# A talking-heads attention with an expert layer: every PSUM place as a tile of its own, given out by the list schedule

## The chip, the cores and the metric

The kernel runs on one core of one Trainium2 chip. The metric is the device time of one execution in microseconds (us); lower is better. A core has five engines with queues of their own: TensorE (PE, matrix products, with its weight loads shown apart as PEld), VectorE (DVE), ScalarE (ACT), GpSimd (POOL) and SyncE (SP, which issues the transfers here). PE writes its products to PSUM, from where DVE and ACT take them; the kernel lays PSUM out as eight banks of 512 fp32 values in each of 128 partitions.

## What is computed

Four batches, 12 heads, 448 tokens, 64 values to a head, and then a feed-forward layer over all 1792 tokens:

```python
scores = scale * np.matmul(q, k.transpose(0, 1, 3, 2))
scores = np.einsum('bhij,hg->bgij', scores, w_pre)
scores = scores - np.max(scores, axis=-1, keepdims=True)
attn = np.exp(scores)
attn = attn / (np.sum(attn, axis=-1, keepdims=True) + 1e-09)
attn = np.einsum('bhij,hg->bgij', attn, w_post)
x = np.matmul(attn, v)          # then (token, head * 64)
...
h = x @ w_in                    # 768 -> 2048
relu6 = np.clip(h + 3.0, 0.0, 6.0)
g = h * relu6 / 6.0
out = g @ w_out                 # 2048 -> 768
```

The two einsums mix the 12 heads before and after the softmax.

## The kernel before

A batch's 448 query rows are cut into chunks of 120, 120, 120 and 90 rows. The work on PE comes in these kinds:

- **scores** (line 327): for each pair of heads, queries times keys into the double bank `pqk`, six pairs to a chunk; ACT copies them out (line 358) and they go through DRAM into the mixing layout `T_all`.
- **pre** (line 421, in `step`): a step is 20 query rows (10 in the last step of a short chunk), as two halves r = 0 and 1 of ten rows. Each half mixes the heads of its scores into one bank of `pp`. DVE takes the row maximum (428), ACT the exponential (429), POOL and DVE the normalization (431, 432, 437). From the second batch on the result is split into two fp16 parts (443, 445, 446).
- **post** (line 455): mixes the heads again, one product group for each half r: 24 matmuls of 60 columns in fp16, 8 in fp32 in the first batch. Both halves use the same place `po`, which is the left halves of two banks of `pz`. ACT evicts half 0 (466) and DVE half 1 (464) into `A`, in runs of five values.
- **av** (492): `A` times the values at a chunk's end, into a double bank of the same ring as the scores' (`pav`).
- **moe1** (612): the first layer of the expert part, 16 groups of 18 matmuls for each of eight token groups (240 or 208 tokens), into one of three half banks of `pz`; ACT (622) and DVE (624) evict a group.
- **across** (272, 274): small reductions over partitions, in another part of `pz`.
- **moe2** (759): the second layer, 24 groups of 48 matmuls, into the banks of `pp`; ACT evicts (764).

The order of all instructions is worked out when the program is built. `Plan` takes every operation with an engine, an estimated duration, what it reads and writes, and a priority; `run` is a list scheduler that goes through estimated time and, whenever an engine is free, takes the ready operation of the best priority. Operations of moe1 and moe2 have late priorities and fill what the others leave. Each engine then executes its list strictly in that order, and waits for what the tiles' readers and writers require. Which place in PSUM a product uses is set before the scheduler runs, by counters (`half`, `bank`) and rings. PSUM has three tiles: `pz` (three banks), `pp` (three banks) and the double bank of `pqk` and `pav`:

```python
    pz = const([P, 3, 2, 256], F32, "pz", psm)
    pp = const([P, 3, 512], F32, "pp", psm)
    banks, wide = [3], [True]
    HALVES = [(2, 0), (0, 1), (2, 1)]
```

For the scheduler each place inside `pz` and `pp` is a buffer of its own (`shared`); for the waits that the program is built with, `pz` is one tile and `pp` is one tile.

Of the kernel before, what the change touches and what calls it, by code (L numbers as in the profile page):

```python
# [48 lines left out]
class Op:  # L49
    __slots__ = ("eng", "dur", "fn", "prio", "n", "succ", "order", "ready", "end", "bytes", "no", "mode")  # L50


class Buf:


    def __init__(self, make, ring=None):
        self.make, self.t, self.uses = make, None, []
        self.prev = self.old = None
# [17 lines left out]

class Plan:
# [11 lines left out]
    def op(self, eng, dur, fn, r=(), w=(), prio=0.0, after=(), nbytes=0, mode=0):  # L89
        o = Op()  # L90
        o.eng, o.dur, o.fn, o.prio, o.bytes, o.mode = eng, dur, fn, prio, nbytes, mode
        o.succ, o.order, o.n, o.ready, o.no = [], [], 0, 0.0, len(self.ops)
# [29 lines left out]
    def run(self):  # L122
# [10 lines left out]
        bw, mode = 0.0, None  # L133
        for o in self.ops:
            if o.eng not in free:
                free[o.eng], wait[o.eng], ready[o.eng] = 0.0, [], []
            if o.n == 0:
                heapq.heappush(wait[o.eng], (0.0, o.no, o))

        def release(s, t):  # L140
            s.ready = max(s.ready, t)
            s.n -= 1
            if s.n == 0:
                heapq.heappush(wait[s.eng], (s.ready, s.no, s))

        while True:
            best = None
            for e in free:
                if ready[e]:
# [10 lines left out]
            while wait[e] and wait[e][0][0] <= t + 1e-9:  # L160
                o = heapq.heappop(wait[e])[2]
                heapq.heappush(ready[e], (o.prio, o.no, o))
            o = heapq.heappop(ready[e])[2]
            if e == "PE" and o.mode != mode:
                same = [x for x in ready[e] if x[2].mode == mode and x[0] < o.prio + self.STAY]
                if same:
                    ready[e].remove(min(same))
                    heapq.heapify(ready[e])
                    heapq.heappush(ready[e], (o.prio, o.no, o))
                    o = min(same)[2]  # L170
# [20 lines left out]
def body(ctx: ExitStack, tc: tile.TileContext, q4, kT, vj, wpre0, wpost0, ident0, w_in, w_out, outT):  # L191
# [55 lines left out]
    HALVES = [(2, 0), (0, 1), (2, 1)]  # L247
    turn = [0]
# [563 lines left out]
```

## Time and profile before

| | before |
|---|---|
| time, median of 3 runs | 1128.89 us (1128.63 to 1132.57) |
| time of the profiled execution | 1122.48 us |
| its span, first to last instruction | 1120.7 us |
| PE busy | 920.3 us (82%) |
| PE weight loads | 682.4 us (61%) |
| ACT, DVE, POOL busy | 476.0 us (42%), 465.6 us (42%), 369.4 us (33%) |
| granted TensorE clock, mean | 0.941 of full speed |

An engine is busy while an instruction of it is shown to execute; the end of a matmul is modelled. PE is the busiest engine by far, but the share is an average over stages that work differently: attention with moe1 between it (to about 755 us), moe1 alone (755 to 855 us), and moe2 (855 us to the end).

### The profile page before, as it was taken

To read this page: it belongs to the slowest core of one execution; us is meant where nothing else is said; L and a number is where in the kernel's file an instruction comes from. 1 tells how busy PE (TensorE), PEld (TensorE's weight loads), DVE (VectorE), ACT (ScalarE), POOL (GpSimd) and SP (SyncE) were. 2 spreads that over 40 slices of the span, in tenths; PEclk is the share of its full clock that TensorE was granted. 3 is DMA by queue.
4 is the path that set the end of the run, shared out by engine and by line. 5 is a ranking of instruction groups with operands and counts; after the bars stand their busy time and mean duration, and the time that the engine had idled before them with its cause. 6 is when DMAs were issued, how large, how long until landed. Compare 5 with 4: busy or idle time off the path is not lost.

```text
span 1120.7 us, 25096 instructions
## 1 busy us (share of the span) xinstructions
PE 920.3 (82%) x10492; PEld 682.4 (61%) x10492; DVE 465.6 (42%) x961; ACT 476.0 (42%) x926; POOL 369.4 (33%) x529
## 2 busy tenths in 40 slices
PE   6878898787887887898887896776668999999997
PEld 1445455554554654555664555665557888888887
DVE  4455656565446367467475565323211020110300
ACT  3454556465556466467564464423212230211200
POOL 1332434166545364466464364512002400000000
PEclk8586789999999999999998999879999999999999
DMA  7785477465466678677776563034213331220300
GB/s 206 200 257 148 148 206 238 140 199 167 107 197 180 186 209 245 185 235 211 230 209 200 172 202 110 18 122 150 69 40 101 97 117 65 78 87 33 115 17 33
DMA packets 80936, 166.07 MB, mean 148 GB/s; under 512 B 7416, under 2 KB 51544, under 8 KB 80824
## 3 DMA queue, kind: packets, MB, share of 16 engines
q1 hardware_dynamic: 80824, 164.48, 49.1%
q8 instruction: 82, 1.34, 0.5%
q14 instruction: 30, 0.25, 0.1%
HBM read 99.27 MB, written 62.60 MB: 144 GB/s over the span
## 4 chain that ended last, share of the span: by engine, by line
PE 56%; ACT 10%; DVE 10%; issue 4%; POOL 1%; DMA 1%; SPq 0%; ACTq 0%; DVEq 0%; POOLq 0%
PE pp L759 22%; PE pz L612 19%; PE pav L492 5%; PE pz L455 4%; ACT rl L622 3%; PE pqk L327 3%; DVE g L624 3%; PE pp L421 2%; ACT e L429 2%; ACT A L466 2%; DVE A L464 2%; DVE nb L428 2%; ACT o L764 1%; DVE eh L443 1%; ACT x L497 1%
## 5 line engine op out<-in xcount | busy, mean ns | idle before, releaser
L612 PE MATMUL pz<-x,wi 128*128 128x208 f16 (+1 forms) x2304 | 254.3, 267 | 60.7 <-DVE g L624 47.2
L612 PEld LDWEIGHTS <-wi 128*128 128x128 f16 x2304 | 218.3, 100 | 103.4 <-issue 91.2
L759 PE MATMUL pp<-g,wo 128*128 128x448 f32 x1152 | 244.3, 372 | 16.9 <-ACT o L764 16.9
L759 PEld LDWEIGHTS pp<-g,wo 128*128 128x128 f32 x1152 | 219.6, 192 | 41.3 <-ACT o L764 25.2
L446 POOL TENSOR_TENSOR el<-e,eh 128x448 f16<-128x448 f32 x135 | 144.2, 1076 | 109.6 <-ACT eh L445 82.9
L437 POOL TENSOR_SCALAR e<-e,r 128x448 f32<-128x448 f32 x180 | 128.4, 725 | 66.6 <-DVE r L432 63.2
L429 ACT ACTIVATE e<-pp,nb 128x448 f32<-128x448 f32 x173 | 108.7, 631 | 70.2 <-DVE nb L428 53.4
L622 ACT ACTIVATE rl<-pz,three,uh 128x240 f32<-128x240 f32 (+1 forms) x128 | 68.8, 537 | 142.6 <-PE pz L612 80.7
L327 PE MATMUL pqk<-ks,qx 64*64 64x448 f32 (+1 forms) x744 | 121.1, 603 | 6.2 <-ACT s L358 5.4
L624 DVE SCALAR_TENSOR_TENSOR g<-rl,six,pz 128x240 f32<-128x240 f32 (+1 forms) x128 | 56.7, 443 | 160.2 <-ACT rl L622 99.6
L455 PEld LDWEIGHTS <-eh 60*128 60x128 f16 x2160 | 57.0, 94 | 108.4 <-issue 107.0
L428 DVE TENSOR_REDUCE nb<-pp 128x1 f32<-128x448 f32 x173 | 101.9, 614 | 35.0 <-ACT e L429 19.6
L421 PE MATMUL pp<-T_all,wpre 64*64 64x448 f32 (+1 forms) x692 | 99.6, 585 | 19.2 <-ACT e L429 10.4
L455 PE MATMUL pz<-wpost_h,eh 60*128 60x60 f16 x1080 | 62.1, 190 | 59.6 <-DVE g L624 23.6
L749 DVE TENSOR_TENSOR g<-gr,g 128x896 fp32r<-128x896 f32 x32 | 34.6, 1091 | 181.4 <-ACT g L748 181.4
L464 DVE TENSOR_SCALAR A<-pz 128x480 f32<-128x480 f32 x88 | 60.0, 682 | 116.2 <-ACT rl L622 63.0
L466 ACT ACTIVATE A<-pz 128x480 f32<-128x480 f32 x92 | 59.8, 650 | 110.4 <-PE pz L612 78.3
L358 ACT ACTIVATE s<-pqk 120x896 f32<-120x896 f32 (+1 forms) x90 | 82.2, 914 | 20.0 <-PE pqk L327 6.8
L455 PEld LDWEIGHTS pz<-wpost_n,e 60*128 60x128 f32 x720 | 55.0, 227 | 46.6 <-issue 24.9
L764 ACT ACTIVATE o<-pp,uo 128x448 f32<-128x448 f32 x24 | 15.1, 634 | 159.0 <-PE pp L759 159.0
L492 PE MATMUL pav<-A,v 128*64 128x120 f32 (+1 forms) x1536 | 81.0, 265 | 1.4 <-ACT A L466 0.7
L492 PEld LDWEIGHTS pav<-A,v 128*64 128x64 f32 x1536 | 76.2, 140 | 5.5 <-issue 2.3
(96 smaller groups left out, 868.4 us busy)
## 6 DMA issues: line engine op xcount, KB each, us to landing
T_all<-sd SPq DMA_DIRECT2D x82, 420.0 KB, 4.5
sd<-s SPq DMA_DIRECT2D x66, 420.0 KB, 5.9
gr<-gd SPq DMA_DIRECT2D x32, 448.0 KB, 3.5
wi<-in_w_in SPq DMA_DIRECT2D x16, 768.0 KB, 4.4
wo<-in_w_out SPq DMA_DIRECT2D x24, 512.0 KB, 8.6
gd<-g SPq DMA_DIRECT2D x32, 240.0 KB, 2.9
sd<-s SPq DMA_DIRECT2D x24, 315.0 KB, 4.9
gd<-g SPq DMA_DIRECT2D x32, 208.0 KB, 3.4
```

Source lines behind the costliest of these rows:

```text
L327: PE.matmul(at[u]()[c:c + m], q()[r, pr, c:c + m], k()[r, pr % 3, :], start=True, stop=True)
L421: PE.matmul(ps[r]()[64 * u:64 * u + 64, :S], wpre8()[rows], T_all()[rows, slot, u], start=True, stop=True)
L428: dve(0.67, lambda r=r: DVE.tensor_reduce(nb()[:, r:r + 1], ps[r]()[:, :S], axis=AX.X, op=ALU.max, negate=True), [ps[r]], [(nb, r)], s + 0 ...
L429: act(0.87, lambda r=r: ACT.activation(e()[:, r], ps[r]()[:, :S], AF.Exp, bias=nb()[:, r:r + 1], accum_out=sm()[:, r:r + 1]), [ps[r], (nb, ...
L437: pool(0.73, lambda r=r: POOL.tensor_scalar(e()[:, r], e()[:, r], rr()[:, r:r + 1], 1.0, op0=ALU.mult, op1=ALU.mult), [rr], [(e, r)], s + ...
L446: pool(1.05, lambda r=r: POOL.tensor_tensor(el()[:, r], e()[:, r], eh()[:, r], op=ALU.subtract), [(e, r), (eh, r)], [(el, r)], s + 0.7 + 0 ...
L455: PE.matmul(pz()[:, u, 0, jc * HR:jc * HR + HR], x()[rows, r, js], w()[rows], start=(i == 0), stop=(i == len(mix) - 1))
L492: PE.matmul(ps()[u * D:(u + 1) * D, run, k:k + n], v()[:, jc, g * D:(g + 1) * D], a()[:, jc * H + g, :n], start=(jc == 0), stop=(jc == NJ ...
L612: PE.matmul(pv(), wi_g[g]()[:, w, f0, cc, :], x()[:, z, cc, :n], start=(cc == 0 and i == 0), stop=(cc == 5 and i == 2))
L622: act(0.57, lambda fc=fc, pv=pv, r=r: ACT.activation(r()[:, :n], pv(), AF.Relu, bias=three()[:, fc:fc + 1], scale=uh()[:, fc:fc + 1]), [ps ...
L624: dve(0.5, lambda fc=fc, pv=pv, r=r, gt=gt: DVE.scalar_tensor_tensor(gt()[:, fc % 2, :n], r()[:, :n], six()[:, fc:fc + 1], pv(), op0=ALU.m ...
L759: PE.matmul(ps()[:, :S], woh[e]()[:, w, fc, :], gs[b, k]()[:, z, fc % 2, :], start=(fc == 0 and i == 0), stop=(fc == NFC - 1 and i == 2))
```

## The change

`Places` is a set of PSUM tiles: one double bank (`pair0`) for the scores and six single banks (`single0` to `single5`) for everything else. A product that needs a place no longer has one assigned by a counter. It says from which set it takes, the scheduler counts it as available only when enough places of the set are free in estimated time, and takes the place that came free first. PE's choice among ready operations is rewritten around that; its rule to stay with the same kind of product within a margin of priority is kept.

Some products change with it. A step's two post halves become one operation that writes two single banks, one for the upper and one for the lower rows (u = 0 and 1); a matmul's 60 results now go to twelve runs of five values with gaps of five between (the other half's values), where they went to 60 adjacent values. ACT evicts the one bank and DVE the other, each when the whole operation is done, in runs of ten. The two halves of an av product and each moe1, moe2 and across product take a single bank of their own. Some entries are added to what a product reads and writes (`(e, "pe")`, `(a, (t, 2))`, `rx`, `(uh, fc)`): in the scheduler's count it then also waits for the buffers that its evictions read or write.

```diff
+class Places:
+
+
+    def __init__(self, makes):
+        self.makes, self.held = makes, [None] * len(makes)
+
+    def free_at(self, i, hop):
+        b = self.held[i]
+        if b is None:
+            return 0.0
+        ends = [u.end for _, u, _ in b.uses]
+        return None if None in ends else max(ends) + hop
+
+    def ready(self, k, hop):
+        t = sorted(x for x in (self.free_at(i, hop) for i in range(len(self.held))) if x is not None)
+        return t[k - 1] if len(t) >= k else None
+
+    def take(self, b, hop):
+        i = min((x, i) for i, x in ((i, self.free_at(i, hop)) for i in range(len(self.held))) if x is not None)[1]
+        self.held[i] = b
+        b.make = self.makes[i]
+
+            if b.pool and not b.uses and b not in o.takes:
+                o.takes.append(b)
...
+        def avail(o):
+            t = o.ready
+            for p in {b.pool for b in o.takes}:
+                x = p.ready(sum(b.pool is p for b in o.takes), self.HOP)
+                if x is None:
+                    return None
+                t = max(t, x)
+            return t
...
+            if e == "PE":
+                at = [(avail(x[2]), x) for x in ready[e]]
+                at = [x for z, x in at if z is not None and z <= t + 1e-9]
+                x = min(at)
+                x = min([z for z in at if z[2].mode == mode and z[0] < x[0] + self.STAY] or [x])
+                ready[e].remove(x)
+                o = x[2]
+                for b in o.takes:
+                    b.pool.take(b, self.HOP)
+            else:
...
-    pz = const([P, 3, 2, 256], F32, "pz", psm)
-    pp = const([P, 3, 512], F32, "pp", psm)
-    banks, wide = [3], [True]
-
-    def shared(ring):
-        return Buf(None, rings.setdefault(("shared", ring), Ring(1)))
-
-    def half():
-        turn[0] = (turn[0] + 1) % len(HALVES)
-        return shared(("ph", turn[0])), HALVES[turn[0]]
-
-    def bank(name):
-        k = banks[0] = (banks[0] + 1) % (4 if wide[0] else 3)
-        z = shared(("pp", k))
-        z.make = (lambda: pz()[:, 2].rearrange("p a b -> p (a b)")) if k == 3 else lambda: pp()[:, k]
+    pairs = Places([const([P, 2, 512], F32, f"pair{i}", psm) for i in range(1)])
+    singles = Places([const([P, 512], F32, f"single{i}", psm) for i in range(6)])
+    mixed = singles
+
+    def place(places):
+        z = Buf(None)
...
+        ps = [place(mixed) for r in range(R)]
...
+        pe(0.85, pre, [T, wpre8], [*ps, (e, "pe")], s - 0.7, mode=1)
...
-            po = shared(("po", 0))
...
+        po = [place(mixed) for u in range(2)]
+        w = G5 * R
+
+        def post():
+            for r in range(R):
...
-                            PE.matmul(pz()[:, u, 0, jc * HR:jc * HR + HR], x()[rows, r, js], w()[rows], start=(i == 0), stop=(i == len(mix) - 1))
+                            out = po[u]()[:, :NJ * H * w].rearrange("p (j g r i) -> p j r g i", j=NJ, g=H, r=R)[:, jc, r]
+                            PE.matmul(out, x()[rows, r, js], z()[rows], start=(i == 0), stop=(i == len(mix) - 1))
+
+        pe(dur * R, post, [x for x, _ in mix] + [z for _, z in mix], [*po, (a, (t, 2))], s + 1.2, mode=2)
+        far = G5 * R
+        for u in range(2):
+            def view(u=u, a=a):
+                return po[u]()[:, :NJ * H * w].rearrange("p (x y) -> p x y", y=w), a()[:, :, i0 + u * far:i0 + u * far + w]
+
+            if u:
+                dve(0.68, lambda view=view: DVE.tensor_scalar(view()[1], view()[0], 2.0 ** -28, None, op0=ALU.mult), [po[u]], [(a, (t, u))], s + 1.4)
             else:
+                act(0.62, lambda view=view: ACT.activation(view()[1], view()[0], AF.Copy, scale=2.0 ** -28), [po[u]], [(a, (t, u))], s + 1.4)
...
+            ps = place(singles)
...
+            pe(2.5, mm, [a, v, rx], [ps, (x, ("pe", c % 2, run))], at + 4 * run, mode=5)
...
-            ps, z = half()
-            pv = lambda z=z: pz()[:, z[0], z[1], :n]
+            ps = place(singles)
+            pv = lambda ps=ps: ps()[:, :n]
...
-            pe(0.0079 * n, mm, [x, *[(wi_g[g], (k, fc)) for k in range(3)]], [ps], at + fc,
-               [u for _, u, _ in rings["shared", ("pp", 3)].all[-1].uses] if (G, fc) in ((0, 0), (0, 1), (0, 2)) else ())
+            pe(0.0079 * n, mm, [x, (uh, fc), *[(wi_g[g], (k, fc)) for k in range(3)]], [ps], at + fc)
...
-        ps = bank(f"po_{b}_{e}")
+        ps = place(singles)
```

Three places show how the order of instructions moves. In the names, `single_84` and the like are the single banks with a running number of the buffer.

The first is PE in the first batch's attention. Before, the post of one step (the rows with `e_424`, eight matmuls for each half) and between its halves a reduction and a score product:

```order
L455 MATMUL pz<-wpost_n,e_424 128x60 x8
L274 LDWEIGHTS ones
L274 MATMUL pz<-top_wi_505,ones 128x1
L327 MATMUL pqk_2_2_536<-ks_0_97,qx_2_168 64x448 x2
L327 MATMUL pqk_2_2_536<-ks_0_97,qx_2_168 56x448 x2
L455 MATMUL pz<-wpost_n,e_424 128x60 x8
```

And after, the last four post matmuls of a step and what follows, the pre product of other steps (`T_all`):

```order
L496 MATMUL single_84<-wpost_n,e_326 128x12x5
L496 MATMUL single_127<-wpost_n,e_326 128x12x5
L458 MATMUL single_156<-T_all,wpre_148 64x448 x2
L458 MATMUL single_136<-T_all,wpre_148 64x448 x2
L458 MATMUL single_154<-T_all,wpre_148 64x448 x2
L458 MATMUL single_134<-T_all,wpre_148 64x448 x2
L309 LDWEIGHTS wist_427
L309 MATMUL single_84<-ident,wist_427 1x128
```

The two halves no longer stand apart with other products between them, the post alternates between two banks, and the pre products and a reduction go to other single banks.

The second is ACT near the end of moe1, where the `rl` of one group follows another. Before:

```order
L622 ACTIVATE rl_8_10800<-pz,three,uh_8254 128x240
L622 ACTIVATE rl_9_10825<-pz,three,uh_8254 128x240
L622 ACTIVATE rl_10_10847<-pz,three,uh_8254 128x240
L622 ACTIVATE rl_11_10869<-pz,three,uh_8254 128x240
L622 ACTIVATE rl_12_10891<-pz,three,uh_8254 128x240
```

And after:

```order
L662 ACTIVATE rl_2_10571<-single_156,three,uh_7792 128x240
L662 ACTIVATE rl_3_10591<-single_84,three,uh_7792 128x240
L662 ACTIVATE rl_4_10615<-single_134,three,uh_7792 128x240
L662 ACTIVATE rl_5_10637<-single_127,three,uh_7792 128x240
L662 ACTIVATE rl_6_10659<-single_136,three,uh_7792 128x240
L662 ACTIVATE rl_7_10681<-single_154,three,uh_7792 128x240
L662 ACTIVATE rl_8_10703<-single_156,three,uh_7792 128x240
```

Each group was read from `pz`; now six banks take turns, and a bank comes back at the seventh group.

The third is PE in moe2, where one pair of groups (`wo_10457`, `wo_10575`) ends and the next begins, with the semaphores that a row waits for. Before:

```order
L759 MATMUL pp<-g_7_12440,wo_10457 128x448 x3
L759 MATMUL pp<-g_7_12440,wo_10575 128x448 x3
L759 MATMUL pp<-g_0_12278,wo_11358 128x448 [waits Activation_49]
L759 MATMUL pp<-g_0_12278,wo_11358 128x448 x2
L759 MATMUL pp<-g_0_12278,wo_11408 128x448 [waits Activation_49]
L759 MATMUL pp<-g_0_12278,wo_11408 128x448 x2
L759 MATMUL pp<-g_0_12278,wo_11358 128x448 x3
```

And after:

```order
L798 MATMUL single_156<-g_7_12340,wo_10137 128x448 x3
L798 MATMUL single_84<-g_7_12340,wo_10273 128x448 x3
L798 MATMUL single_134<-g_0_12178,wo_11258 128x448 x3
L798 MATMUL single_127<-g_0_12178,wo_11308 128x448 x3
L798 MATMUL single_134<-g_0_12178,wo_11258 128x448 x3
L798 MATMUL single_127<-g_0_12178,wo_11308 128x448 x3
```

The first matmul of each group of the new pair waited for ACT; after the change no wait stands there, and the banks are others than those of the pair that ends.

## Rows read from the trace of the kernel before

**Rows 1.** Stages: from:to, length, PE, PEld, DVE, ACT, POOL busy, clock, DMA share, GB/s.

```profile
0.00:755.00 755.00, 612.37 (x8729) 405.84 (x8730) 417.51 (x896) 402.50 (x816) 339.90 (x507) 0.92 0.62 182
755.00:855.40 100.40, 63.78 (x613) 57.14 (x613) 21.32 (x39) 25.36 (x44) 9.16 (x8) 1.00 0.27 84
855.40:1120.70 265.30, 244.14 (x1153) 219.39 (x1151) 26.80 (x26) 48.12 (x66) 20.36 (x16) 0.97 0.24 76
```

**Rows 2.** Timeline in the second stage: start, length, engine, line, operation, [idle before, releaser].

```profile
776.33 2.00 PE L612 MATMUL pz<-x,wi 128*128 128x240 f16 x18 [1.14 <-DVE g L624]
...
778.37 0.55 ACT L622 ACTIVATE rl<-pz,three,uh 128x240 f32<-128x240 f32 x1 [1.76 <-PE pz L612]
778.95 0.47 DVE L624 SCALAR_TENSOR_TENSOR g<-rl,six,pz 128x240 f32<-128x240 f32 x1 [1.22 <-ACT rl L622]
779.47 2.00 PE L612 MATMUL pz<-x,wi 128*128 128x240 f16 x18 [1.14 <-DVE g L624]
```

**Rows 3.** Waits of PE, 150 to 755 us: total, times, longest.

```profile
PE pz L455 <- DVE g L624: 24.3, 32, 1.7
PE pz L455 <- ACT A L466: 22.2, 29, 1.3
PE pz L612 <- DVE g L624: 10.6, 13, 1.6
PE pp L421 <- ACT e L429: 10.2, 11, 1.9
PE pz L612 <- DVE A L464: 7.5, 8, 1.9
PE pz L455 <- DVE A L464: 6.0, 7, 1.2
PE pz L455 <- ACT rl L622: 5.9, 7, 1.9
PE pz L612 <- ACT rl L622: 4.8, 8, 0.7
```

**Rows 4.** Waits of PE in the last stage.

```profile
PE pp L759 <- ACT o L764: 16.9, 22, 0.8
```

**Rows 5.** Timeline in the last stage, where one pair of products ends.

```profile
875.63 0.88 PE L759 MATMUL pp<-g,wo 128*128 128x448 f32 x3 [0.72 <-ACT o L764]
```

**Rows 6.** Windows inside the first stage: its start, one dense stretch, the rest.

```profile
0.00:150.00 150.00, 117.45 (x935) 62.92 (x937) 84.17 (x201) 72.93 (x131) 50.81 (x101) 0.75 0.67 196
150.00:200.00 50.00, 44.03 (x518) 31.55 (x516) 27.65 (x66) 28.38 (x52) 17.96 (x35) 0.93 0.70 212
150.00:755.00 605.00, 494.93 (x7798) 342.92 (x7795) 333.34 (x697) 329.57 (x686) 289.09 (x406) 0.96 0.61 179
```

**Rows 7.** Timeline of one step's two post products in the first stage.

```profile
320.72 0.20 PE L455 MATMUL pz<-wpost_h,eh 60*128 60x60 f16 x2 [0.63 <-DVE g L624]
...
321.02 0.21 PE L455 MATMUL pz<-wpost_h,el 60*128 60x60 f16 x2
...
321.16 1.78 PE L612 MATMUL pz<-x,wi 128*128 128x208 f16 x18
...
322.97 0.65 ACT L466 ACTIVATE A<-pz 128x480 f32<-128x480 f32 x1 [2.79 <-PE pz L612]
...
323.67 0.20 PE L455 MATMUL pz<-wpost_h,eh 60*128 60x60 f16 x2 [0.74 <-ACT A L466]
```

**Rows 8.** Windows of line 455 alone on PE, first stage.

```profile
0.00:755.00 755.00, 130.78 (x3960) 0.92 0.62 182
```

**Rows 9.** Groups by form: count, busy us, mean ns, idle before and releasers.

```profile
L464 DVE TENSOR_SCALAR A<-pz 128x480 f32<-128x480 f32 x88 | 60.0, 682 | 116.2 <-ACT rl L622 63.0 <-PE pz L612 29.0 <-PE pz L455 15.5
L466 ACT ACTIVATE A<-pz 128x480 f32<-128x480 f32 x92 | 59.8, 650 | 110.4 <-PE pz L612 78.3 <-PE pz L455 11.4 <-DVE top_wi L273 4.5
...
L343 DVE COPY s<-pqk 120x448 f32<-120x448 f32 x3 | 1.9, 625 | 6.6 <-ACT s L342 6.5
L342 ACT ACTIVATE s<-pqk 120x448 f32<-120x448 f32 x3 | 1.6, 544 | 5.7 <-PE pqk L327 4.1 <-DVE s L343 1.6
```

More of the change, by code (lines that the diff above doesn't have):

```diff
@@ L49 @@
 class Op:
-    __slots__ = ("eng", "dur", "fn", "prio", "n", "succ", "order", "ready", "end", "bytes", "no", "mode")
+    __slots__ = ("eng", "dur", "fn", "prio", "n", "succ", "order", "ready", "end", "bytes", "no", "mode", "takes")
 class Buf:
@@ L91, in op @@
         o.eng, o.dur, o.fn, o.prio, o.bytes, o.mode = eng, dur, fn, prio, nbytes, mode
-        o.succ, o.order, o.n, o.ready, o.no = [], [], 0, 0.0, len(self.ops)
+        o.succ, o.order, o.n, o.ready, o.no, o.end, o.takes = [], [], 0, 0.0, len(self.ops), None, []
         deps = {}
@@ L133, in run, with push @@
         bw, mode = 0.0, None
+        def push(o):
+            if o.eng == "PE":
+                ready["PE"].append((o.prio, o.no, o))
+            else:
+                heapq.heappush(wait[o.eng], (o.ready, o.no, o))
         for o in self.ops:
@@ L137, in run @@
             if o.n == 0:
-                heapq.heappush(wait[o.eng], (0.0, o.no, o))
+                push(o)
         def release(s, t):
@@ L148, in run @@
             for e in free:
-                if ready[e]:
+                if e == "PE":
+                    at = [(avail(x[2]), x) for x in ready[e]]
+                    at = [(x, z) for x, z in at if x is not None]
+                    if not at:
+                        continue
+                    t = max(free[e], min(at)[0])
+                elif ready[e]:
                     t = free[e]
@@ L159, in run @@
             t, e = best
[L160 to L168, printed above, removed]
+            if e == "PE":
+                at = [(avail(x[2]), x) for x in ready[e]]
+                at = [x for z, x in at if z is not None and z <= t + 1e-9]
[5 more added lines that the diff above has]
+                    b.pool.take(b, self.HOP)
+            else:
+                while wait[e] and wait[e][0][0] <= t + 1e-9:
+                    o = heapq.heappop(wait[e])[2]
                     heapq.heappush(ready[e], (o.prio, o.no, o))
-                    o = min(same)[2]
+                o = heapq.heappop(ready[e])[2]
             o.end = t + o.dur
@@ L243, in body @@
     ones = const([1, P], BF16, "ones")
[L244 to L264 removed]
+    pairs = Places([const([P, 2, 512], F32, f"pair{i}", psm) for i in range(1)])
[3 more added lines that the diff above has]
+        z = Buf(None)
+        z.pool = places
+        return z
     def across(src, name, prio):
[L268 to L271 removed]
+        slot = place(singles)
+        top = const([1, 1], BF16, f"top_{name}")
+        row = lambda: slot()[:1, :P]
+        out = lambda: slot()[:, P:P + 1]
         pe(0.15, lambda: PE.matmul(row(), src().bitcast(BF16)[:, 1:2], ident(), start=True, stop=True), [src, ident], [(slot, 0)], prio, mode=3)
@@ L332, in first_scores @@
         q, k = qs[0, 0], ks[0, pr // 3]
-        if pr % 2:
-            ps = [bank(f"ppre_s{pr}_{u}") for u in range(2)]
+        if pr % 3:
+            ps = [place(singles) for u in range(2)]
             at2 = [lambda u=u: ps[u]()[:, :S] for u in range(2)]
         else:
-            two = pair(f"pqk_0_0_{pr}")
+            two = place(pairs)
             ps = [(two, 0), (two, 1)]
@@ L354, in scores @@
         sd, q, k = s_dram[b, c], qs[b, c], ks[b, pr // 3]
-        ps = pair(f"pqk_{b}_{c}_{pr}")
+        ps = place(pairs)
         pe(0.85, products(q, k, pr, n, [lambda u=u: ps()[:, u, :S] for u in range(2)]), [(k, pr % 3), q], [ps], at, mode=1)
@@ L414, in step @@
                 T_all()[4:4 + HR * R, slot], sd()[i0:i0 + 10 * R].rearrange("(u r) h j -> (r h) u j", u=2)), [sd, T_all], [T], s - 2.5)
-        ps = [bank(f"ppre_{s}_{r}") for r in range(R)]
+        ps = [place(mixed) for r in range(R)]
         def pre():
@@ L446, in step @@
                 pool(1.05, lambda r=r: POOL.tensor_tensor(el()[:, r], e()[:, r], eh()[:, r], op=ALU.subtract), [(e, r), (eh, r)], [(el, r)], s + 0.7 + 0.3 * r)
-                mix, dur = [(eh, wpost_h), (eh, wpost_l), (el, wpost_h)], 0.47
-            def post(r=r, mix=mix):
+        if s < POST16:
+            mix, dur = [(e, wpost_n)], 0.62
+        else:
+            mix, dur = [(eh, wpost_h), (eh, wpost_l), (el, wpost_h)], 0.47
+        po = [place(mixed) for u in range(2)]
+        w = G5 * R
@@ L637, in body @@
     for _ in range(10):
-        PE.matmul(pp()[:, 0], warm[:, :P], warm, start=True, stop=True)
+        PE.matmul(singles.makes[0]()[:, :], warm[:, :P], warm, start=True, stop=True)
     mixes()
```

39 lines of the change are left out of this document (10 added, 29 removed).

## The prediction

> **What bounds the kernel now.** I read the windows by stage first, because a share over the whole span hides where PE stands still [rows 1]. PE is busy for 612.4 of the first 755 us, for 63.8 of the next 100.4 us, and for 244.1 of the last 265.3 us. No other engine comes near: in the first stage DVE has 417.5 us and ACT 402.5 us. So the end is set by PE's work and by what PE waits for, and a change that alters no amount of work can win only PE's idle time: 142.6, 36.6 and 21.2 us.
>
> Then I looked for the reason of each, beginning where only one kind of work runs. In the second stage moe1 has PE for itself. Its groups start every 3.14 us, do 2.00 us of matmuls, and before each PE stands 1.14 us "<-DVE g" [rows 2]. In that gap ACT and DVE evict the group just finished. But three half banks take turns (line 248), and the next group writes to another one: with three places it should start at once. It waits for every reader of `pz`, whichever part they read. The waits thus follow the tile, not the place, and that is what the reader is to see in these four rows: a stall of exactly one eviction, with other places free.
>
> The same is seen in the first stage. The list of waits of PE from 150 to 755 us [rows 3] names lines 455, 612 and 421, and the releasers are evictions of other products in the same tile: a post waits for a moe1 eviction (24.3 us) and moe1 for a post's (7.5 us). The one row of another kind is the post that waits for ACT's line 466 (22.2 us): both halves of a step really share one place. The eight rows add up to 91.5 us, of 110.1 us that PE is idle there (605 less 494.9, [rows 6]). What is behind it stands in the timeline of one step [rows 7]: ACT's eviction of half 0 could have begun after 321.2 us, but a moe1 group had been issued into `pz` in the meantime and the eviction waited for it too (2.79 us idle), then half 1 waited 0.74 us for the eviction. Line 466 lost 78.3 us in all behind moe1 [rows 9]. In the third stage the first products of a pair of groups wait for the last pair's evictions, 22 times, 16.9 us [rows 4, 5].
>
> **The change, part by part.**
>
> *moe1 alone.* After the change the order rows show six single banks in turn, and a group's place was last read six groups earlier. The 1.14 us go, and PE is left with its own 63.8 us: -36.6 us [rows 1]. (613 matmuls are 34 groups of 18.) I see nothing that is late next: ACT takes 0.55 and DVE 0.47 us to a group [rows 2], against 2 us of PE. The new order has more groups than these 34 behind the last av product (46). That moves work from one stretch to another and is neither gain nor loss, if PE has no holes.
>
> *moe2.* The order rows show no wait left at the start of a pair: -16.9 us [rows 4]. The other 4.3 us of idle time stay.
>
> *Attention with moe1.* At most all 91.5 us go [rows 3]; PE would then be busy for 96% of the stretch (494.9 of 513.5). But what waited for a place will in part wait for data, since PE comes to each product earlier, and the step's chain through DVE, ACT and POOL takes as long as before. For the lower end I take the share that PE reached with the old waits in a dense 50 us, 44.0 of 50 or 88% [rows 6]: 494.9/0.88 = 562 us, or -43 us. I take the middle, -67 us. The first 150 us, with 32.5 us of idle time [rows 6], I leave as they are: the waits of [rows 3] begin behind them.
>
> *The post products.* Two things pull in opposite directions. The results of a matmul now go to runs of five with gaps. No matmul in the trace writes so, and the price can lie anywhere from nothing to a doubling of line 455's 130.8 us [rows 8]; twelve pairs start within 0.30 us here, 27 ns for 60 columns, so there is no slack inside the group that would hide it [rows 7]. The nearest rows are the evictions, which write runs of five: ACT takes 650 ns for 480 values against 544 ns for 448 adjacent ones, 11% more for each value, and DVE 682 against 625 ns, 2% [rows 9]. Of 130.8 us that is 3 to 14 us. I take 8 us. On the other side the 180 post operations become 92, and 88 changes of kind disappear on PE; between the last post pair and the moe1 group that follows lie 0.14 us instead of 0.03 [rows 7], so 88 times 0.11, some 10 us. Together I take them for zero.
>
> [...]
>
> *The evictions* of the posts now both wait for the whole operation. Nothing waits for them but av at the chunk's end and the place, and the step takes places of its own. Their number stays, 184 for 180.
>
> *Transfers.* The same bytes go in less time. The DMA engines are busy for 62% of the first stage [rows 1]; with 67 us less it is 68%, and single stretches already have 67 and 70% [rows 6]. I price it at nothing.
>
> [...]
>
> **The sum.** 1120.7 - 36.6 - 16.9 - 67 + 0 = 1000.2 us of span. The profiled execution took 1122.48 us, 1.8 more than its span, which gives 1002.0; the median of the runs, 1128.89, is 0.57% above that execution, so 1008 us.
>
> **The rivals.**
>
> *Attention is held by data.* If the step's chain, not the places, sets its pace, each wait removed in [rows 3] comes back under another name, and only the other two stages gain: (1120.7 - 53.5 + 1.8) x 1.0057 = 1075 us. For it: POOL alone has 289 us of work in the 605 and each step goes through four engines. Against it: apart from places, PE's list of waits holds hardly anything after 150 us (91.5 of 110.1 in eight rows), and a stock of moe1 groups is there to fill.
>
> [...]
>
> [...]
>
> *The tiles change nothing*, as the waits belong to something else than the tile: 1129 us. The rotating half banks of [rows 2] speak against it.
>
> **Chances.** The forecast 0.69; its own range, from all of the 91.5 us with 10 us saved on posts to -43 us with 14 us lost, is 973 to 1046 us. Attention held by data 0.12, post dearer by half or more 0.08 (half of these short of slower than before), better clock 0.08, nothing 0.03. To leave out no more than 2 in 10 the range goes from 958 us (most of the clock's case) to 1065 us (some of the data's). Half a per cent is about what a measurement of this kernel can tell from no change. Faster by more: 0.69 + 0.12 + 0.08 + 0.04 = 0.93; within it 0.03; slower 0.04.
>
> **What would show it.** Right, step by step: moe1 groups at the end follow each other without idle time, at 1.9 us on average (63.8 us for 34); the waits of the moe2 products on ACT are gone; in the attention stretch no post waits for a moe1 eviction, and PE's share is above 88%. Wrong: waits of the same total for POOL, DVE or transfers in that stretch (data); a spacing of the post pairs well above 27 ns (gaps in the output); the same 1.14 us gaps (the tile was not the cause). The forecast is wrong by most if the new order keeps the step's chain from running ahead, since then moe1 is left to the end while PE waits in the attention part.

## The result and the profile after

The changed kernel takes 896.51 us in the median of 4 runs (890.31 to 896.78), beside 1130.73 us of the kernel before: 0.791 of its time (95% interval 0.788 to 0.795). The forecast was 1008 us with a range from 958 to 1065. The direction held, the size did not: the gain is 234 us where 121 were forecast.

The profiled execution took 890.31 us with a span of 888.5 us; before, they were 1122.48 and 1120.7. From the page: the engine totals and the rows over 40 equal slices.

```profile
PE 866.8 (98%) x10492; PEld 666.6 (75%) x10492; DVE 470.7 (53%) x965; ACT 467.3 (53%) x926; POOL 385.9 (43%) x529
...
PE   7899899999999999999999999999999999999998
PEld 1366387776666767567766687999999999999997
DVE  4477858887458698578698778452210210301100
ACT  4457748777578767767867666562333221302210
POOL 1245636587667677567577668330035000000000
PEclk9579879999999999999999999999999999999999
```

PE is busy for 98% of the span instead of 82%, the other engines do the same work as before in less time, and the granted clock is below 0.90 only within the first six slices; from 150 us on its mean is 1.00. The windows by stage answer to [rows 1] and the first row of [rows 6] (from:to, length, PE, PEld, DVE, ACT, POOL busy, clock, DMA share, GB/s). The last av product is issued at 574.2 us, and moe1 alone lasts until 652.25.

```profile
0.00:150.00 150.00, 135.55 (x1272) 77.78 (x1273) 100.22 (x240) 88.03 (x164) 65.41 (x123) 0.82 0.79 242
150.00:574.47 424.47, 420.78 (x7244) 296.57 (x7242) 316.28 (x648) 297.90 (x639) 289.47 (x383) 1.00 0.77 235
574.47:652.25 77.78, 77.78 (x829) 76.44 (x830) 27.81 (x54) 33.92 (x61) 10.87 (x8) 1.00 0.41 126
652.25:888.50 236.25, 232.69 (x1152) 215.80 (x1151) 26.38 (x25) 47.40 (x65) 20.14 (x16) 1.00 0.27 85
```

Between 150 and 574 us PE stands still for 3.7 us of 424; before it was 110.1 of 605. What PE still waits for in the whole span (total us, times, longest) answers to [rows 3, 4]:

```profile
PE pair L364 <- ACT s L395: 6.2, 9, 1.1
PE single L458 <- DMA T_all<-s: 5.1, 5, 1.5
PE single L496 <- POOL el L480: 1.6, 3, 0.7
...
PE single L653 <- ACT e L466: 0.2, 1, 0.2
```

Of evictions of another product one is left, 0.2 us of a moe1 group behind an exponential. The row on L395 is a real one: the scores' double bank is a single place. The others shown are data. The chain that ended last runs through PE alone from the last av product on (start, length, what):

```profile
574.47 77.78 PE single L653 x828
652.25 232.11 PE single L798 x1149
```

The timeline of moe1 alone, beside [rows 2]: 83 matmuls in one row with no idle time between groups, while ACT evicts a group behind them.

```profile
594.83 8.37 PE L653 MATMUL single<-x,wi 128*128 128x208 f16 x83
...
595.48 0.53 ACT L662 ACTIVATE rl<-single,three,uh 128x208 f32<-128x208 f32 x1 [0.24 <-PE single L653]
```

To compare stages, like work has to stand together: 34 moe1 groups were left for the stage alone before, 46 now. The matmuls of the stage by their columns (count, busy us, mean ns), before and then after, show 16 groups of 240 columns in both; the 12 more are groups of 208:

```profile
L612 PE MATMUL pz<-x,wi 128*128 128x240 f16 x288 | 32.1, 266 | 18.1 <-DVE g L624 18.1
L612 PE MATMUL pz<-x,wi 128*128 128x208 f16 x324 | 31.8, 252 | 19.7 <-DVE g L624 19.7
```

```profile
L653 PE MATMUL single<-x,wi 128*128 128x208 f16 x540 | 48.5, 253 | 0.0
L653 PE MATMUL single<-x,wi 128*128 128x240 f16 x288 | 29.7, 266 | 0.0
```

At 48.5/30 = 1.62 us each the 12 are 19.4 us, which I count to attention: 574.5 + 19.4 = 593.9 us now for what took 755.

| stage, like work | before | after | change | forecast |
|---|---|---|---|---|
| attention with 94 moe1 groups | 755.0 | 593.9 | -161.1 | -67 |
| of that PE idle | 142.6 | 18.1 | -124.5 | |
| of that PE busy | 612.4 | 575.7 | -36.6 | |
| 34 moe1 groups alone | 100.4 | 58.4 | -42.0 | -36.6 |
| moe2 | 265.3 | 236.2 | -29.1 | -16.9 |
| span | 1120.7 | 888.5 | -232.2 | -120.5 |

So of some 112 us that the forecast lacked, 94 lie in one term.

### The profile page after: what moved, and what is told of

It reads as the page before. It is cut to its first block, busy times and chain, and to the rows that moved or that the text cites. A ratio compares the mean times of both kernels' runs of the same rounds, so it can differ in the third digit from the quotient of the medians.

```text
span 888.5 us, 24968 instructions
## 1 busy us (share of the span) xinstructions
PE 866.8 (98%) x10492; PEld 666.6 (75%) x10492; DVE 470.7 (53%) x965; ACT 467.3 (53%) x926; POOL 385.9 (43%) x529
## 4 chain that ended last, share of the span: by engine, by line
PE 88%; DMA 4%; DVE 2%; ACT 2%; POOL 1%; issue 1%; ACTq 0%; POOLq 0%; DVEq 0%
PE single L798 26%; PE single L653 24%; PE single L496 12%; PE pair L364 10%; PE single L533 8%; PE single L458 7%; DMA sd<-s 3%; ACT s L395 1%; DMA wi<-in_w_in 1%; POOL el L480 1%; PE single L678 0%; ACT e L466 0%; POOL e L474 0%; DVE A L505 0%; DVE nb L465 0%
## 5 line engine op out<-in xcount | busy, mean ns | idle before, releaser
L653 PE MATMUL single<-x,wi 128*128 128x208 f16 (+1 forms) x2304 | 233.5, 260 | 0.8 <-issue 0.7
L798 PE MATMUL single<-g,wo 128*128 128x448 f32 x1152 | 232.9, 364 | 0.0
L798 PEld LDWEIGHTS single<-g,wo 128*128 128x128 f32 x1152 | 216.1, 188 | 16.5
L466 ACT ACTIVATE e<-single,nb 128x448 f32<-128x448 f32 x180 | 112.9, 631 | 28.0 <-DVE nb L465 25.7
L364 PE MATMUL pair<-ks,qx 64*64 64x448 f32 (+1 forms) x736 | 114.7, 582 | 6.7 <-ACT s L395 6.2
L465 DVE TENSOR_REDUCE nb<-single 128x1 f32<-128x448 f32 x180 | 104.5, 614 | 31.1 <-PE single L458 29.8
L458 PE MATMUL single<-T_all,wpre 64*64 64x448 f32 (+1 forms) x720 | 97.7, 583 | 5.1 <-DMA T_all<-s 5.1
L395 ACT ACTIVATE s<-pair 120x896 f32<-120x896 f32 (+1 forms) x90 | 82.4, 915 | 36.3 <-PE pair L364 14.6
L533 PEld LDWEIGHTS single<-A,v 128*64 128x64 f32 x1536 | 75.6, 139 | 7.6 <-issue 3.6
L533 PE MATMUL single<-A,v 128*64 128x120 f32 (+1 forms) x1536 | 79.9, 264 | 0.0
```

The lines of the kernel that those rows point to most:

```text
L364: PE.matmul(at[u]()[c:c + m], q()[r, pr, c:c + m], k()[r, pr % 3, :], start=True, stop=True)
L395: act(0.97, lambda: ACT.activation(st()[:n], ps()[:n, :, :S], AF.Copy), [ps], [st], at + 0.5)
L458: PE.matmul(ps[r]()[64 * u:64 * u + 64, :S], wpre8()[rows], T_all()[rows, slot, u], start=True, stop=True)
L465: dve(0.67, lambda r=r: DVE.tensor_reduce(nb()[:, r:r + 1], ps[r]()[:, :S], axis=AX.X, op=ALU.max, negate=True), [ps[r]], [(nb, r)], s + 0 ...
L466: act(0.87, lambda r=r: ACT.activation(e()[:, r], ps[r]()[:, :S], AF.Exp, bias=nb()[:, r:r + 1], accum_out=sm()[:, r:r + 1]), [ps[r], (nb, ...
L533: PE.matmul(ps()[u * D:(u + 1) * D, k:k + n], v()[:, jc, g * D:(g + 1) * D], a()[:, jc * H + g, :n], start=(jc == 0), stop=(jc == NJ - 1))
```

## The experiments

Two explanations of the gain stand against each other. One is the prediction's: waits follow the tile, so tiles of their own remove them (A). The other is that the new order, with places given out while it is made, brings the gain (B). Beside them were the price of the gaps in the post's output, the worth of joining the halves, the number of places, and the question whether data is the next limit.

**The changed order with one tile.** The order of instructions and the places stay as in the changed kernel; the six single banks are slices of one tile.

```diff
-    singles = Places([const([P, 512], F32, f"single{i}", psm) for i in range(6)])
+    bank6 = const([P, 6, 512], F32, "bank6", psm)
+    singles = Places([lambda i=i: bank6()[:, i] for i in range(6)])
```

> The changed kernel with its order of instructions unchanged, but the six single banks are slices of one tile again. Theory A (the waits follow the tile, and they alone held PE): PE waits for evictions of other products again, the 1.1 us before each of the 46 moe1 groups at the end come back (some 50 us) and so do the waits in attention (over 100 us); 1060 to 1150 us. Theory B (the gain in attention is that of the new order: places given by the scheduler, joined posts, PE's rewritten choice): the order is still the new one, so only the end and moe2 lose, some 70 us; 950 to 980 us.

Measured: 1580.51 us, 1.398 of before (1.395 to 1.402). PE's waits (us, times, longest), and one moe1 group near the end:

```profile
PE bank L497 <- ACT e L467: 73.3, 34, 3.6
PE bank L654 <- DVE g L665: 61.9, 51, 2.7
...
PE bank L799 <- ACT o L804: 16.9, 22, 0.8
```

```profile
1253.36 2.00 PE L654 MATMUL bank<-x,wi 128*128 128x240 f16 x18 [1.14 <-DVE g L665]
```

The 1.14 us of [rows 2] are back to the hundredth, with six banks in turn, and so are the 22 waits and 16.9 us of [rows 4]. The direction is A's. The size missed both expectations: before had three tiles, this has two, and the new order counts on free places everywhere, so that a post waits for the exponential of another step (73.3 us). The granted clock is 0.82 in the mean beside 0.97 in the changed kernel, and PE's busy time for the same instructions is 1080 us beside 867. The new order is worth nothing without the tiles; it is worse than the old.

**The old order with more tiles.** The kernel before, order and places unchanged; `pp` becomes three tiles, and the third bank of `pz` a tile of its own. The first two banks of `pz` stay one tile, since a post's two halves use both at once.

```diff
-    pz = const([P, 3, 2, 256], F32, "pz", psm)
-    pp = const([P, 3, 512], F32, "pp", psm)
+    pz01 = const([P, 2, 2, 256], F32, "pz", psm)
+    pz2 = const([P, 2, 256], F32, "pz2", psm)
+    pps = [const([P, 512], F32, f"pp{i}", psm) for i in range(3)]
```

> The kernel before with its order and its places unchanged, but the three banks of pp are three tiles, and the third bank of pz (two of the three moe1 halves) is a tile of its own; the first two banks of pz stay one tile for post, across and the third moe1 half. Theory A: most waits of pre, moe1 and moe2 for other products go, those inside the two shared banks stay; 960 to 1040 us. Theory B: the old order does not profit in attention; the end (two of three groups) and moe2 gain some 25 and 17 us; 1070 to 1095 us.

Measured: 966.24 us, 0.855 of before (0.853 to 0.857). What PE waits for longest in it, and ACT's evictions of a post half (count, busy, mean ns, idle before and releasers):

```profile
PE pz L456 <- ACT A L467: 12.3, 17, 0.8
PE pz L613 <- DVE g L625: 8.1, 13, 1.2
PE pz L456 <- DVE A L465: 6.2, 7, 1.0
```

```profile
L467 ACT ACTIVATE A<-pz 128x480 f32<-128x480 f32 x92 | 59.9, 651 | 59.7 <-PE pz L613 25.7 <-PE pz L456 20.8 <-DVE top_wi L274 5.4
```

With three more tiles and no instruction moved, 164 of the 234 us are there. B fails as the main cause. What stays in front are waits in the part that is still one tile. ACT stands behind moe1 (line 613 here) for 25.7 us where it was 78.3 in [rows 9]. This kernel alone gains 43 us more than the forecast had for the whole change, so the effect of the tiles itself was taken too small.

**Places in a fixed turn.** The six tiles stay; the scheduler hands them out in a fixed turn, where it took the one that came free first.

```diff
     def take(self, b, hop):
-        i = min((x, i) for i, x in ((i, self.free_at(i, hop)) for i in range(len(self.held))) if x is not None)[1]
+        i = self.turn
+        self.turn = (i + 1) % len(self.held)
...
```

> The changed kernel with the six single banks given out in turn instead of the one that came free first; a product still counts as available only when its places are free. Theory A (tiles of their own are what counts): no change, 890 to 905 us. Theory B (which place is given matters): products with long evictions block the turn, PE's idle time comes back in attention; 930 us or more.

Measured: 902.90 us, 0.799 (0.794 to 0.803). The interval overlaps that of the change; by the medians the free choice is worth 6 us. Between the old order with more tiles (966 us) and the change lie 70 us. What the free choice leaves of them belongs, then, to the places that are still one tile there, to six places common to all kinds, and to an order made for them. The runs don't split these further.

**Four single banks.** Two of the eight banks lie idle.

```diff
-    singles = Places([const([P, 512], F32, f"single{i}", psm) for i in range(6)])
+    singles = Places([const([P, 512], F32, f"single{i}", psm) for i in range(4)])
```

> The changed kernel with four single banks instead of six (two banks stay unused). Theory A (separate tiles do it, their number matters little as long as a step's pre and post, two banks each, and one moe1 group find a place): 900 to 930 us. Theory C (the gain needs all six places): PE is idle again for places, 960 us or more.

Measured: 918.27 us, 0.813 (0.808 to 0.817), 22 us above the change. PE is still busy for 96%: the last av product moves from 574.2 to 652.1 us, and moe1 fills the time. With fewer places the steps advance more slowly, but PE hardly stands still.

**Adjacent results.** The post's 60 results go to adjacent places again; the evictions take them apart in runs of five, as before.

```diff
-                            out = po[u]()[:, :NJ * H * w].rearrange("p (j g r i) -> p j r g i", j=NJ, g=H, r=R)[:, jc, r]
+                            out = po[u]()[:, (r * NJ + jc) * HR:(r * NJ + jc + 1) * HR]
...
```

> The changed kernel with the post products' 60 results adjacent again, the halves r = 0 and 1 behind each other in the bank; the evictions take them apart and write runs of five again. If the gaps cost (24 pairs start 36 ns apart after the change, 27 ns before): 135 halves in fp16 times 12 pairs times 9 ns are 14 us less, as PE is busy for 98%; 880 to 885 us. If the spacing comes from something else, no change: 894 to 899 us. The evictions take some 70 ns more each on ACT, which is off the path in both.

Measured: 887.09 us, 0.782 (0.778 to 0.787), 9.4 us below the change and 2 us above the expectation. First and last of a step's 24 pairs of post matmuls, first in the changed kernel (start, length), then in this one:

```profile
554.14 0.21 PE L496 MATMUL single<-wpost_h,eh 60*128 60x60 f16 x2
...
554.96 0.21 PE L496 MATMUL single<-wpost_h,el 60*128 60x60 f16 x2
```

```profile
403.36 0.20 PE L496 MATMUL single<-wpost_h,eh 60*128 60x60 f16 x2
...
404.00 0.19 PE L496 MATMUL single<-wpost_h,el 60*128 60x60 f16 x2
```

23 intervals take 0.82 us with gaps and 0.64 us without: 36 against 28 ns a pair. Over all fp16 pairs of the two traces the median is 34 against 28 ns; the fp32 pairs of the first batch start 112 ns apart in both, and all of them together are busy for 53.8 us with gaps and 55.4 us without. The same in sum: line 496's busy time in the changed kernel, then in this one.

```profile
0.00:900.00 900.00, 123.50 (x3960) 0.97 0.60 185
```

```profile
0.00:900.00 900.00, 112.92 (x3960) 0.96 0.60 185
```

The gaps cost 10.6 us of PE, and PE is busy for 97 to 98% of the span in both, so nearly all of it is in the time. The evictions give a little of it back in the changed kernel, where they write runs of ten: 581 and 652 ns against 650 and 682 in [rows 9].

```profile
L505 DVE TENSOR_SCALAR A<-single 128x480 f32<-128x480 f32 x88 | 57.4, 652 | 44.2 <-PE single L496 42.0 <-PE single L311 1.2 <-PE single L309 0.9
...
L507 ACT ACTIVATE A<-single 128x480 f32<-128x480 f32 x88 | 51.1, 581 | 36.3 <-PE single L496 36.3
```

**Two post operations.** The halves are scheduled as two operations again; tiles, gaps and evictions stay as changed.

```diff
-        pe(dur * R, post, [x for x, _ in mix] + [z for _, z in mix], [*po, (a, (t, 2))], s + 1.2, mode=2)
+        for r in range(R):
+            pe(dur, lambda r=r: post(r), [(x, r) for x, _ in mix] + [z for _, z in mix],
+               [*[(p, r) for p in po], (a, (t, 2, r))], s + 0.9 + 0.3 * r, mode=2)
...
```

> The changed kernel with a step's post as two operations again, one for each half, into the same two banks; the evictions still wait for both. If joining the halves is part of the gain (88 fewer changes of kind on PE at some 0.11 us, and no half that keeps two banks while it waits for the other): 905 to 915 us. If only the tiles count: 892 to 900 us.

Measured: 894.39 us, 0.790 (0.786 to 0.794): no difference from the change. Joining the halves is worth nothing that these runs can tell.

**One place for moe2.** The groups of the last stage all use the double bank's first half.

```diff
     def moe2(b, e):
-        ps = place(singles)
+        ps = place(pairs)
...
```

> The changed kernel with moe2 in the first half of the one double bank, so that each of its 24 groups waits for the eviction of the one before. Theory A with the waits alone: 23 gaps of 0.7 to 0.8 us, 17 us more, 912 to 915 us. Theory E (a gap on PE also costs clock behind it, which is why PE's busy time for moe2 fell from 244 to 233 us): also some 11 us of busy time, 922 to 927 us, with stretches of granted clock below 1.00 behind the gaps.

Measured: 932.54 us, 0.824 (0.820 to 0.828), 36 us above the change and beyond both expectations. PE's waits in it, and two groups of 48 matmuls:

```profile
PE pair L798 <- ACT o L803: 18.2, 23, 1.0
...
PE pair L798 <- ACT g L787: 3.8, 6, 1.2
PE pair L798 <- DVE g L788: 3.4, 8, 0.5
```

```profile
736.14 12.03 PE L798 MATMUL pair<-g,wo 128*128 128x448 f32 x48 [0.77 <-ACT o L803]
748.95 9.88 PE L798 MATMUL pair<-g,wo 128*128 128x448 f32 x48 [0.77 <-ACT o L803]
```

The 18.2 us stand where one place makes the next group wait for the eviction, nearly as in [rows 4]. Not foreseen were 7.2 us of waits for `g`: with one place two groups no longer interleave, so a group asks for its next operand sooner (this is argued, not tested). Line 798 is busy for 246.1 us instead of 232.9. Most of the groups that run through take 9.87 or 9.88 us, 0.17 more than the 9.70 on average in the changed kernel (232.9/24). A matmul of line 798 is shown there for 364 ns on average and adds 202 ns (232.9/1152): the other 0.16 us of a group's last matmul, which the next group covers there, stand alone here. Two groups take 12.03 and 11.30 us. More on that at the end.

**Lighter moe1, in both kernels.** Each moe1 group does 6 of its 18 matmuls. This asks what holds attention when PE has less to fill it with.

```diff
-                    for i, (w, z) in enumerate(((0, 0), (1, 0), (0, 1))):
-                        PE.matmul(pv(), wi_g[g]()[:, w, f0, cc, :], x()[:, z, cc, :n],
-                                  start=(cc == 0 and i == 0), stop=(cc == 5 and i == 2))
+                    PE.matmul(pv(), wi_g[g]()[:, 0, f0, cc, :], x()[:, 0, cc, :n], start=(cc == 0), stop=(cc == 5))
```

> The changed kernel with 6 instead of 18 matmuls in each moe1 group (only the high parts of weights and values are multiplied; everything else stays). It takes 128 x 12 matmuls of some 0.1 us from PE, 145 to 155 us. Theory A (PE's own work is the bound, data are there in time): the time falls by all of it, to 740 to 755 us, and PE stays above 95% busy. Theory D (the attention steps' data set the pace just behind PE): less than 100 us are won, 800 us or more, with PE waiting for ACT, DVE, POOL or transfers.

> The kernel before with 6 instead of 18 matmuls in each moe1 group, as h_light_after. If PE's work bounds the kernel before too: 150 us less, 975 to 985 us. Theory A (the chain through the shared tiles sets the pace, of which the moe1 matmuls are a link, since evictions wait for them too): the matmuls count at least in full, and the waits stay at some 100 us or more; 950 to 990 us with PE busy for less than 80%.

One execution of each: 836.43 us (span 834.6) in the changed kernel's version, 1038.32 (1036.5) in that of before. PE's waits in the first, then in the second:

```profile
PE single L652 <- DVE g L662: 15.4, 14, 3.4
PE pair L364 <- ACT s L395: 12.9, 20, 1.7
PE single L496 <- POOL el L480: 8.6, 20, 0.7
```

```profile
PE pz L611 <- DVE g L622: 48.0, 43, 3.4
PE pz L455 <- ACT A L466: 24.5, 30, 1.6
```

In the changed kernel two thirds of moe1's matmuls left out save 54 us of span, as the second expectation had it (less than 100); PE falls to 91%, and the last av product comes at 548.7 us instead of 574.2. So with much less work on PE the steps come only about 26 us sooner: another limit lies close behind PE's work, but the changed kernel does not reach it. That it is data alone is not shown. Up to 549 us the longest waits are those for the scores' one double bank (12.9 us) and for POOL's `el` (8.6), and the granted clock of that stretch is lower than in the changed kernel, 0.91 beside 0.95. The 15.4 us of moe1 behind DVE lie almost wholly after it, in moe1 alone.

In the kernel before, the span falls by 84 us, less than either expectation had, and the tile's waits stay as they were: moe1 behind its eviction 48.0 us (47.2 over the whole span of the kernel before), the post behind ACT 24.5 (23.0). The mean granted clock is 0.855 there beside 0.941, and PE's busy time falls by only 94 us.

**Fewer places, and full rows.** Two versions on top of the adjacent results. The first has two double banks and four single ones:

```diff
-    pairs = Places([const([P, 2, 512], F32, f"pair{i}", psm) for i in range(1)])
-    singles = Places([const([P, 512], F32, f"single{i}", psm) for i in range(6)])
+    pairs = Places([const([P, 2, 512], F32, f"pair{i}", psm) for i in range(2)])
+    singles = Places([const([P, 512], F32, f"single{i}", psm) for i in range(4)])
```

> The changed kernel with adjacent post results (as e2_adjacent, 887 us), two double banks for the scores and four single banks. The longest wait of PE left after the change is that of the scores for ACT's eviction of the one double bank, 6.2 us in 9 times. If places for the scores are what is left to win: 878 to 884 us. If the singles are the scarcer: above 890 us.

Measured: 929.08 us, 0.821 (0.817 to 0.825). The second double bank does not take the scores' wait for L395 away: it is 12.8 us in 10 times, beside 6.2 in 8 with the adjacent results alone. Fewer single banks are not the whole loss either, since four of them beside one double bank took 918.27 us, with the gaps. Why the second double bank costs time is open.

The second lets the 90-row chunks of scores compute all 120 rows, so that their second column part is 56 wide instead of 26:

```diff
-            for c in range(0, n, D):
-                m = min(D, n - c)
+            for c in range(0, CI, D):
+                m = min(D, CI - c)
...
```

> Adjacent post results (e2_adjacent, 887 us) and, in the chunks of 90 rows, score products over 120 rows as in the others (the rows behind the 90th are zeros in the input and are not read). In the trace a pair takes 1.8 us in the 90-row chunks (parts of 64 and 26 columns) and 1.0 us in the others (64 and 56). With PE as the bound 24 pairs at 0.8 us give 19 us: 865 to 872 us. If PE is not the bound there: 880 us or more.

Measured: 873.37 us, 0.772 (0.767 to 0.776): the fastest version, 23 us below the change and 1 us above the expectation. Two groups of eight score matmuls in the changed kernel, the first of a 120-row chunk, the second of a 90-row one (start, length; a row names the form of its first matmul), then line 364's busy time with adjacent results alone, and with full rows too:

```profile
206.34 0.98 PE L364 MATMUL pair<-ks,qx 64*64 64x448 f32 x8
...
214.79 1.84 PE L364 MATMUL pair<-ks,qx 64*64 64x448 f32 x8
```

```profile
0.00:900.00 900.00, 118.48 (x768) 0.96 0.60 185
```

```profile
0.00:900.00 900.00, 101.60 (x768) 0.96 0.60 185
```

More columns are computed in less time: -16.9 us of PE. A group with parts of 64 and 56 columns takes 0.98 us, one with 64 and 26 takes 1.84: in the first the second part starts 0.01 us after the first part, in the second 0.90 us after it, so the two no longer run beside each other. That was in both kernels (0.98 and 1.84 us before too) and was never part of the change.

## Why the prediction was wrong in its size

**The cause held.** "The waits thus follow the tile, not the place": the same places in one tile bring back each of the three stalls, and the old order with more tiles loses most of them. The four signs named for "right" are all there: no idle time between moe1 groups, no wait of moe2 for ACT, no post behind a moe1 eviction, and PE at 99% from 150 to 574 us.

**The step that failed is the attention term**, -67 us where -161 came. It was the middle of two shares of PE, chosen because "what waited for a place will in part wait for data, since PE comes to each product earlier, and the step's chain through DVE, ACT and POOL takes as long as before". Three things are wrong in it:

- *The reason.* Data waits are a few us after the change (5.1 for `T_all`, 1.6 for `el`), and with the lighter moe1 the steps end earlier than PE lets them end now (548.7 us beside 574.2), so data did not hold them. The step's chain did not take as long as before: it was itself held by the tile. [Rows 9] had that, and the prediction quoted it: ACT's evictions stood 78.3 us behind moe1 matmuls that they didn't need; 25.7 us of it are left with the old order and more tiles, nothing in the changed kernel. A wait for the tile on ACT or DVE delays the next data as well, so that removing it lets data come sooner (argued from these rows). The upper bound of 91.5 us was no bound either: it took the eight longest rows of the list, and of the 18.6 us in the rest some 9 are waits for evictions of other products too. From 150 us on, idle time fell by 106.4 us of 110.1. That is 39 us beyond the -67.
- *The start.* "The first 150 us [...] I leave as they are": its idle time went from 32.5 to 14.5 us, another 18. The waits there mostly name data before (5.5 us of posts for POOL's `e` is the longest group), and that row is gone after. The old order with more tiles alone brings PE's busy time in this window from 117.5 to 128.0 us (135.6 in the changed kernel), so a part of these data waits followed from tiles too.
- *The busy time.* "A change that alters no amount of work can win only PE's idle time": PE's busy time in the attention part fell by 36.6 us with the same work. In moe1 alone, at a granted clock of 1.00 before and after, 34 groups fell from 63.8 to 58.4 us of busy time: the end of a group's last matmul, which nothing covered before, now lies beside the next group. A matmul of 240 columns is shown for 266 ns in both and adds 103 ns to the busy time now (29.7/288), which leaves 0.16 us a group. The 94 groups in attention would by that give up to 15 us, an estimate. The clock is the other part: 0.75 became 0.82 in the first 150 us, and 0.96 became 1.00 behind them. In moe2 of the kernel before, 93 matmuls take 18.87 us at a clock of 1.00 and 20.47 at 0.92, nearly the same product. Busy time times clock, a rough estimate from the windows, is 563 us before and 551 after, which would put some 25 of the 36.6 us on the clock and 12 on everything else, the gaps' price included. No run splits them.

39 + 18 + 37 are the 94 us.

**moe1 alone**, -36.6 forecast, -42.0 measured: the gaps went as said, and the 5.4 us are the overlap just told. **moe2**, -16.9 forecast, -29.1 measured: idle time fell by 17.6 us, and busy time by 11.5 us. The clock's 0.97 became 1.00, which by the same estimate is some 7 us of 244. The rest fits the uncovered ends of the groups: 0.17 us each in the run with one place, which is 4 us for the 22 gaps of [rows 4], an estimate.

**The posts** were counted +8 for the gaps and -10 for joining. The gaps cost 9.4 us; joining gave nothing. The size taken from the evictions was nearly right by luck: the spacing of the fp16 pairs rose by 21% in the median (by 29% in the step shown), not by 2 to 11%, but 1620 pairs of 28 ns are only 45 of the 112.9 us of line 496, and 6 ns more on each are 10 us, against 10.6 measured. The fp32 pairs, 112 ns with gaps and without, show no loss.

**The rivals.** Attention held by data (1075 us) is refuted by the waits left, tiles that change nothing (1129 us) by the 896.51 us, and posts dearer by half or more by the 10.6 us that the gaps cost, where half of [rows 8] would be 65. The better clock of the chances was nearest: some 25 us in attention and 7 in moe2, both by the estimate above, came in addition to the forecast's own terms. No run shows the clock's case from which the range takes its 958 us; in the first 150 us the clock rose from 0.75 to 0.82, not to 1.00.

## What to carry to other kernels

Where a wait names an eviction of another product in the same tile, cut the tile before touching the order: it costs a few lines, and a good order without the tiles was worse here than the old one (1580.51 us beside 1130.73). Such waits also held an evicting engine here (ACT for 78.3 us), and without them the last av product came at 574.2 us instead of 750.2, so don't take a part of PE's waits off for data before an experiment with less work on PE has shown that data is late; and count the whole list of waits, not its longest rows. A gap at the end of a group cost more than its idle time here: the uncovered end of the last matmul (0.16 us a moe1 group), and, behind four of the eleven pairs of gaps in moe2, a mean clock of 0.92 over the next 93 matmuls.

## What was unexpected of the hardware

The granted clock fell to 0.78 behind two short gaps. In the last stage of the kernel before, two stalls of less than 0.8 us stand 1.7 us apart. The third row is the last such place of the stage (start, length, matmuls, idle time before them):

```profile
896.90 0.88 PE L759 MATMUL pp<-g,wo 128*128 128x448 f32 x3 [0.79 <-ACT o L764]
898.55 20.47 PE L759 MATMUL pp<-g,wo 128*128 128x448 f32 x93 [0.77 <-ACT o L764]
...
1097.61 18.87 PE L759 MATMUL pp<-g,wo 128*128 128x448 f32 x93 [0.77 <-ACT o L764]
```

In windows from these stalls on, and in one right behind two later stalls of 0.78 and 0.77 us, the clock is the first number behind the engines:

```profile
895.00:900.00 5.00, 3.44 (x13) 2.48 (x12) 0.00 (x0) 1.27 (x2) 0.00 (x0) 0.88 0.24 92
900.00:905.00 5.00, 5.00 (x21) 4.55 (x20) 1.09 (x1) 1.30 (x2) 0.00 (x0) 0.78 0.00 1
905.00:910.00 5.00, 5.00 (x27) 4.69 (x26) 2.18 (x2) 1.56 (x2) 0.00 (x0) 1.00 0.65 184
...
945.00:950.00 5.00, 5.00 (x23) 4.63 (x22) 0.00 (x0) 0.00 (x0) 0.00 (x0) 0.84 0.00 0
```

At 900 to 905 us PE is busy for all of the 5 us and gets a clock of 0.78; 21 matmuls fit where 27 do five us later. Not every such pair of stalls is followed by it: after the 0.72 us of [rows 5] and a second stall of 0.72 us the clock stays at 1.00 from 875 to 885 us. Of the eleven pairs of stalls in that stage, four are followed by 93 matmuls in 20.5 to 21.0 us at a mean clock of 0.92, the others by 93 in 18.9 to 19.1 at 1.00, as in the third row. With one place for moe2, most groups behind a single gap of 0.77 us take 9.87 us. The two long ones, 12.03 and 11.30 us, each come right after a row of short gaps in which PE waited for `g` and the eviction; the mean clock from 700 us on is 0.98, where it is 1.00 from 660 to 700 us. A third such row of gaps, before 875 us, was followed by a group of 10.01 us by the chain that ended last, which has 12.05 and 11.32 for the two long ones. In the changed kernel, without the gaps, the last stage has a mean of 1.00. What decides it in each case is open.
